# Layer 0 of a linear-attention block: tiles 6 and 7 are turned by VectorE and DMA instead of TensorE

## The chip, the core and the metric

The kernel runs on one core of one Trainium2 chip. The metric is the device time of one execution in microseconds (us). Before the change the median of three runs is 867.65 us (867.58 to 867.68). A core has five engines that run their own instruction streams in order and wait for each other by semaphores: TensorE (PE in the profile, its weight loads shown as PEld), VectorE (DVE), ScalarE (ACT), GpSimd (POOL) and SyncE (SP). In this kernel nearly every DMA is issued from SP's queue (SPq in the profile), in program order.

## What is computed

Two layers, each an attention block and an MLP block on x of 2048 rows by 448 columns:

```python
for layer in range(2):
    n = layernorm(x);  q, k, v = n @ wqkv          # 16 heads of 28
    pq, pk = phi(q), phi(k)                        # t + 1 if t > 0 else exp(t), + 1e-6
    x = x + (pq @ (pk.T @ v) / (pq @ sum(pk))) @ wo    # per head
    n = layernorm(x)
    x = x + gelu(n @ w1 + b1) @ w2 + b2
```

All inputs are float32. The kernel keeps that precision by splitting each operand into a high part (rounded to fp32r) and a low part (the rest), and sums three products: high by high, high by low, low by high.

## The kernel before, in words

The rows are cut into 16 tiles of 128 (t = 0 to 15) and 4 blocks of 4 tiles. A layer has a first phase, `phase1`, which goes over the tiles and gathers pk and G = n.T @ pk; a short transition; then the MLP, into which the second half of the attention is woven. The order of all instructions is written by hand: each engine and each queue executes its share in the order in which the Python code emits it. The change touches only phase 1 of layer 0.

For a tile t phase 1 needs these steps, each a token in the strings of `STEPS` and `STEP` and a function of the same meaning:

- `a` (`stage_a`, lines 206 to 216): statistics of the row norm on VectorE, then an inverse root on GpSimd (`brs`).
- `n` (`stage_n`, line 423): normalise on VectorE, in place. If t < TURNED[l], ScalarE also copies the last 64 columns twice into a tail (line 427), which the TensorE transposes read.
- The tile must be turned so that the 448 columns lie on partitions. There are two ways. For t < TURNED[l], `T` (`stage_b`, `transpose_x`, line 259) makes four TensorE transposes into a PSUM bank, and `X` (`split_x`, lines 271 and 272) splits it: ScalarE writes the high part XH, VectorE the low part XL. For t >= TURNED[l], `v` or `tu` (`stage_t`, `turn`, lines 298 and 299) turns squares of 32 by 32 on VectorE into a buffer `sq` that holds two tiles. After the odd tile of the pair, `store_sq` (line 304) writes the buffer to DRAM. The token `sp` (`spread`, line 310) reads it back with four DMAs that put each square in its place, and `X` (`split_t`, lines 316 and 317) splits from SBUF. The four reads wait for the store.
- `K` (`stage_k`, line 334): 11 matmuls XH, XL by wk into `psk`. `kp`, `kh`, `kl` (lines 350 to 353, 492, 501, 508): phi, its high and low part, and the running sum `za`.
- `s` (lines 458 to 460): high and low part of the normalised tile in its own layout, `xnh` and `xnl`.
- `G` (`stage_g`, line 563): 11 matmuls for the tile before.
- `Q` (`stage_q`, line 334): 11 matmuls by wq into `psq`, for t up to 8 in this phase. `qp` (`stage_qphi`, lines 350 to 353, 536): phi of it, one step later, and a store. The PSUM banks of `psq` and of the TensorE transposes are the same two (tag `h`).
- `ld`: loads of x for later tiles; `bg`: one or two pieces of the MLP weights are loaded by SP and split by ScalarE and GpSimd (lines 381 to 393).

In step t the token `K` works on tile t, `T` and `X` on tile t + 1, `G` on tile t - 1, `Q` on tile t, and `qp` on the tile whose `Q` ended the step before. The default order of a step is `qp K T X s a kp n kh kl tu G bg Q ld sp`. Below, K(12) stands for the token K of tile 12, and so on. Step 3 begins on TensorE at 27.14 us with K(3), step 4 at 34.33, step 5 at 41.42, step 6 at 48.49, step 7 at 55.54, step 8 at 62.16, step 9 at 68.76, step 10 at 73.16, step 11 at 77.57 and step 12 at 81.98.

Before the change tiles 8 to 15 of layer 0 are turned by VectorE: tiles 8 and 9 in step 4, tile 10 in step 5, and so on to tile 15 in step 10. The store of a pair follows its odd tile; the spreads are issued at the end of steps 4, 6, 8 and 10; the splits X(8) and X(9) stand in steps 7 and 8, X(10) and X(11) in steps 9 and 10, X(12) in step 11.

`k_at`, `q_at` and `g_at` say at which of the 11 places of a group the products with a low part stand.

Of the kernel before, what the change touches and what calls it, by code (L numbers as in the profile page):

```python
# [22 lines left out]
def linear_attn_mlp_kernel(  # L23
# [12 lines left out]
    pe, act, dve, pool, sp = nc.tensor, nc.scalar, nc.vector, nc.gpsimd, nc.sync  # L36
# [8 lines left out]
    G = 112  # L45
# [37 lines left out]
    def load_x(l, t):  # L83
        xt[l, t] = t448("H", 8, f"x{l}_{t}")
        sp.dma_start(xt[l, t], x_d[l][t * 128:(t + 1) * 128, :])
# [161 lines left out]
    def block(key):  # L247
        if key not in blocks:
            blocks[key] = Block(APART if key[0] == "a" else 0)
        return blocks[key]  # L250
# [3 lines left out]
    def transpose_x(xn, tail, key, j, tag="m"):  # L254

        block(key)
        tp = tps[key, j] = bank(tag, 4 if tag == "acc" else 2, "tp")
        for c in range(4):
            pe.transpose(tp[:, c * 128:(c + 1) * 128], xn[:, c * 128:(c + 1) * 128] if c < 3 else tail, ident)
# [8 lines left out]
    def split_x(key, j):  # L268
        tp = tps.pop((key, j))
        hi, lo = blocks[key].pieces(j)  # L270
        act.copy(hi, tp)
        dve.tensor_sub(lo, tp, f(hi))
# [20 lines left out]
    def turn(x, key, t):  # L293
        x = x[:, :D]
        if (key, t // 2) not in squares:
            squares[key, t // 2] = half("sq")
        sq = squares[key, t // 2].rearrange("p (m c u n) -> p c m u n", m=4, c=4, n=32)[:, :, :, t % 2]
        dve.transpose(sq[:, :3], x[:, :TL].rearrange("p (c m n) -> p c m n", c=3, n=32))
        dve.transpose(sq[:, 3].rearrange("p (u m) n -> p u m n", u=2),
                      x[:, TL:].rearrange("p (m n) -> p m n", n=32)[:, None].to_broadcast([128, 2, 2, 32]))  # L300
# [56 lines left out]
    def bg_pieces():  # L357
        n = 0
        both = []

        def stage():
            nonlocal n
            n += 1
            if n <= LATE:
                k = (n - 1) // 2
                if k % 2 == 0 or k > 5:
                    return t512("xn", 2, "stg")[:, :D]

                if n % 2:
                    both.append(half("stg"))  # L370
                return both[-1][:, n % 2 * 512:][:, :D]
            return t448(f"W{5 + n % 2}", 1, "stg")

        for fc in range(4):
            sl = slice(fc * D, (fc + 1) * D)
            for c in range(4):
                s = stage_piece(w1[:, sl], c, sp, stage())

                def go(c=c, s=s, sl=sl):
                    if c < 3:  # L380
                        act.copy(w1h[:, c, sl], s)
                        pool.tensor_tensor(w1l[:, c, sl], s, f(w1h[:, c, sl]), op=OP.subtract)
                    else:
                        act.copy(w1x[:, sl], s)
                        pool.tensor_tensor(w1x[64:128, sl], s[64:128], f(w1x[64:128, sl]), op=OP.subtract)
                yield go
        for i in range(NF):
            s = stage()
            sp.dma_start(s, w2[i * 128:(i + 1) * 128, :])

            def go(i=i, s=s):
                act.copy(w2h[:, i], s)
                pool.tensor_tensor(w2l[:, i], s, f(w2h[:, i]), op=OP.subtract)
            yield go

    bg = bg_pieces()
# [14 lines left out]
    sts = {}  # L411


    TURNED = (8, 0)
    tails = {}

    def stage_a(l, t):
# [2 lines left out]
    def stage_n(l, t):  # L420
# [3 lines left out]
        xns[l, t] = xs  # L424
        if t < TURNED[l]:
            d = tails[l, t] = b2b[:, t % 2 * 128:][:, :128]
            act.copy(d.rearrange("p (u n) -> p u n", u=2), xs[:, None, TL:].to_broadcast([128, 2, 64]))

    def stage_t(l, t):
        if t >= TURNED[l]:  # L430
            turn(xns[l, t], ("a", l, t // 4), t % 4)
            if t % 2:
                store_sq(("a", l, t // 4), t % 4 // 2)

    def stage_sp(l, t):
        if t >= TURNED[l]:
            block(("a", l, t // 4))
            spread(("a", l, t // 4), t % 4 // 2)

    def stage_b(l, t, tag="h"):  # L440
        if t < TURNED[l]:
            transpose_x(xns[l, t], tails.pop((l, t)), ("a", l, t // 4), t % 4, tag)
# [4 lines left out]
    def stage_x(l, t):  # L447
        key = ("a", l, t // 4)
        if t < TURNED[l]:
            split_x(key, t % 4)  # L450
# [13 lines left out]

    def k_at(l, t):
        if t < 9:
            return (3, 6, 9, 11) if t == 0 or l == 0 and 2 < t < 8 else (2, 5, 8, 11)
        return (2, 5, 8, 11) if t == 9 else (1, 4, 7, 10)

    def q_at(l, t):  # L470
        if t < 9:
            return (2, 5, 8, 11) if l == 0 and t < 7 else (2, 4, 7, 10) if t == 0 else (1, 4, 7, 10)
        return {11: (4, 7, 10, 11), 12: (5, 7, 9, 11),
                13: (5, 8, 10, 11), 15: (1, 5, 8, 11)}.get(t, (1, 4, 7, 10))

    def g_at(l, t):
        if t < 9:
            return (4, 7, 10) if l == 0 and 0 < t < 6 else (3, 6, 9)
        return (2, 5, 8) if t < NT - 1 else (2, 6, 9)

    def stage_k(l, t, cs=range(4)):
        ko[l, t] = proj("k", ("a", l, t // 4), t % 4, ko.get((l, t)), cs, k_at(l, t))
# [41 lines left out]
    def stage_q(l, t, cs=range(4), tag=None):  # L524
        if tag:
            qs_[l, t] = bank(tag, 4, "psq")[:, :D]
        qs_[l, t] = proj("q", ("a", l, t // 4), t % 4, qs_.get((l, t)), cs, q_at(l, t))
        if 3 in cs:
            qo.append((l, t, qs_.pop((l, t))))

    def stage_qphi(n=9):
        for _ in qo[:n]:
            l, t, o = qo.pop(0)

            e = phi(o, "eq", tag="e" if t < NT - 2 else "E")
            sp.dma_start(pq_d[l][t * 128:(t + 1) * 128, :], e)

    def fill_qphi():

        l, t, o = qo.pop(0)  # L540
        e = t512("e", 3, "eq")[:, :D]
        p = t512("E", 2, "ep")[:, :D]
        act.activation(e, o, AF.Relu, scale=-1.0)
        act.activation(p, o, AF.Relu)
        act.activation(e, e, AF.Exp, scale=-1.0)
        pool.tensor_tensor(e, p, e, op=OP.add)
        sp.dma_start(pq_d[l][t * 128:(t + 1) * 128, :], e)

    def stage_g(l, t, acc, mid=lambda: None):
        h, lo = split.pop((l, t))  # L550
        kh, kl = ks.pop((l, t))
        first, last = t == 0, t == NT - 1
        x = [h[:, c * 128:(c + 1) * 128] for c in range(3)] + [h[:, TL:]]
        his = [(c, x[c], k) for c in range(4) for k in (kh, kl)]
        if t == NT - 3:
            his = his[::2] + his[1::2]
        los = [(c, lo[:, c * 128:(c + 1) * 128], kh) for c in range(3)]
        made = merge(his, los, g_at(l, t))
        for i, (c, w, k) in enumerate(made):
            if i == 3:  # L560
                mid()
            others = [m[0] for m in made[:i]], [m[0] for m in made[i + 1:]]
            pe.matmul(acc[c], w, k, start=first and c not in others[0], stop=last and c not in others[1])  # L563
# [19 lines left out]
    STEP = "qp K T X s a kp n kh kl tu G bg Q ld sp"  # L583
    STEPS = {
# [9 lines left out]
    }  # L594
# [117 lines left out]
    def trans_gt(tr, acc):  # L712
        tr.gt = []
        for c in range(4):
            s = t512("A" if c < 2 else "B", 2, "gt")[:, :D]
            act.copy(s, acc[c])
            tr.gt.append(s)
# [52 lines left out]
    def load_pq(l, b, j):  # L770
        t = b * 4 + j
        pqt[l, t] = t448(f"W{j}", 1, f"pq{l}_{t}")
        sp.dma_start(pqt[l, t], pq_d[l][t * 128:(t + 1) * 128, :])
# [245 lines left out]
    for l in range(LAYERS):  # L1019
# [11 lines left out]
        def pre(j):  # L1031
# [6 lines left out]
            Q=lambda j: stage_q(l, fill.pop(0)), Qp=lambda j: fill_qphi(), Qv=lambda j: stage_qphi(j or 9),  # L1038
            Qa=lambda j: stage_q(l, fill.pop(0), tag="acc"), G=lambda j: stage_g(l, NT - 1, acc, lambda: trans_z(tr, zs[l])),
            ld=lambda j: (load_pq(l, 0, j), load_x(l, j)), gt=lambda j: trans_gt(tr, acc),  # L1040
# [14 lines left out]
        for b in range(NB):  # L1055
# [6 lines left out]
            for i in range(NF):  # L1062
# [12 lines left out]
                elif l + 1 < LAYERS:  # L1075
# [4 lines left out]
                    if i in (3, 4, 6, 7, 8):  # L1080
                        t = (3, 4, 6, 7, 8).index(i)
# [36 lines left out]
```

## Time and profile before

| | |
|---|---|
| median of three runs | 867.65 us |
| profiled execution | 867.87 us, of which the span is 866.1 us |
| TensorE matmul busy | 861.0 us, 99% of the span |
| VectorE, ScalarE, GpSimd busy | 494.3, 344.0, 216.5 us |
| granted TensorE clock | 1.00 |
| DMA | 94.76 MB, 109 GB/s mean |

The profile gives times from the start of the span; the 1.77 us between the span and the execution's own time lie around it. A row of the timeline has the start, the duration, the engine, the line of the kernel, the operation, output and input, how many instructions were merged into the row, and in brackets how long the engine had stood idle before it and who released it. Matmuls overlap, so that the pitch from one start to the next, and not the duration, is what one of them costs.

### The profile page before, as it was taken

Reading aid. Unit: us, or ns where it says so; the run is one execution under the profiler, and the core shown is the slowest. Engines: PE = TensorE matmul, PEld = TensorE weight load, DVE = VectorE, ACT = ScalarE, POOL = GpSimd, SP = SyncE. Lnnn points to the kernel's source line nnn. Section 1 sums busy time; section 2 is a strip of 40 time slices with the busy share of each in tenths; the row PEclk is TensorE's granted clock in tenths of the full one; section 3 lists DMA queues with packets and bytes.
Section 4 is the critical chain, followed back from the end, with each engine's and each line's share of the span. In section 5 each row is a group of like instructions: output and inputs, shape, how many; then the busy total and the mean of one; then the engine's idle time right before and its main releaser. Section 6 shows DMA issues by size and latency. Waiting matters only on the chain.

```text
span 866.1 us, 11660 instructions
## 1 busy us (share of the span) xinstructions
PE 861.0 (99%) x4181; PEld 771.3 (89%) x4181; DVE 494.3 (57%) x962; ACT 344.0 (40%) x604; POOL 216.5 (25%) x246
## 2 busy tenths in 40 slices
PE   9999999999999999999999999999999999999998
PEld 8999988888888888888899998988888888888887
DVE  7888596659456443226477876864674483533112
ACT  6776635334323322333356665432232233223231
POOL 5566522235013112012222343120220140140000
PEclk9999999999999999999999999999999999999999
DMA  5475636533313402051146443252332423111001
GB/s 160 139 235 177 192 89 215 184 105 116 134 60 107 156 0 98 1 181 49 49 141 194 164 129 107 100 189 81 113 109 92 135 71 116 50 49 43 0 1 43
DMA packets 63642, 94.76 MB, mean 109 GB/s; under 512 B 8928, under 2 KB 58720, under 8 KB 63584
## 3 DMA queue, kind: packets, MB, share of 16 engines
q1 hardware_dynamic: 63408, 93.87, 33.6%
q8 instruction: 33, 0.54, 0.2%
q14 instruction: 25, 0.20, 0.1%
q10 hardware_dynamic: 176, 0.14, 0.0%
HBM read 56.17 MB, written 34.60 MB: 105 GB/s over the span
## 4 chain that ended last, share of the span: by engine, by line
PE 98%; DMA 0%; DVE 0%; ACT 0%; POOL 0%; issue 0%; SPq 0%; DVEq 0%; ACTq 0%
PE hp L889 32%; PE y L919 10%; PE y L918 10%; PE y L920 10%; PE G L563 8%; PE psq L334 8%; PE psk L334 8%; PE op L827 2%; PE op L826 2%; PE op L828 2%; PE op L816 1%; PE op L815 1%; PE op L817 1%; PE kvp L724 1%; PE mp L734 1%; PE op L830 1%
## 5 line engine op out<-in xcount | busy, mean ns | idle before, releaser
L895 DVE TENSOR_TENSOR gl<-g,gh 128x512 fp32r<-128x512 f32 x112 | 83.2, 743 | 293.5 <-ACT gh L894 293.5
L891 ACT ACTIVATE g<-hp,b1s 128x512 f32<-128x512 f32 x112 | 77.2, 689 | 399.9 <-PE hp L889 395.4
L919 PE MATMUL y<-w2l,gh 128*128 128x448 f32 x447 | 163.6, 366 | 0.0
L918 PE MATMUL y<-w2h,gh 128*128 128x448 f32 x447 | 162.0, 362 | 0.0
L920 PE MATMUL y<-w2h,gl 128*128 128x448 f32 x447 | 160.1, 358 | 0.0
L889 PE MATMUL hp<-XH,w1l 128*128 128x512 f32 x336 | 130.7, 389 | 0.0
L889 PE MATMUL hp<-XH,w1h 128*128 128x512 f32 x336 | 130.7, 389 | 0.0
L889 PE MATMUL hp<-XL,w1h 128*128 128x512 f32 x336 | 130.1, 389 | 0.0
L216 POOL TENSOR_TENSOR brs<-bve,mhalf 128x1 f32<-128x1 f32 x64 | 39.5, 617 | 281.7 <-DVE bve L214 281.3
L918 PEld LDWEIGHTS y<-w2h,gh 128*128 128x128 f32 x447 | 83.7, 187 | 9.4
L919 PEld LDWEIGHTS y<-w2l,gh 128*128 128x128 f32 x447 | 83.9, 188 | 7.0
L920 PEld LDWEIGHTS y<-w2h,gl 128*128 128x128 f32 x447 | 84.0, 188 | 5.1 <-DVE gl L895 0.2
L889 PEld LDWEIGHTS hp<-XL,w1h 128*128 128x128 f32 x336 | 63.1, 188 | 13.1
L889 PEld LDWEIGHTS hp<-XH,w1h 128*128 128x128 f32 x336 | 63.0, 187 | 10.7
L889 PEld LDWEIGHTS hp<-XH,w1l 128*128 128x128 f32 x336 | 63.1, 188 | 9.9
L894 ACT CAST gh<-g 128x512 fp32r<-128x512 f32 x112 | 69.7, 623 | 3.6
L334 PE MATMUL psk<-wk,XH 128*128 128x448 f32 x210 | 61.8, 364 | 0.0
L334 PE MATMUL psq<-wq,XH 128*128 128x448 f32 x210 | 61.3, 366 | 0.0
L777 POOL TENSOR_TENSOR pz<-pq,zb 128x448 f32<-128x448 f32 x32 | 36.9, 1155 | 90.8 <-DVE dn L783 69.3
L459 POOL TENSOR_TENSOR xnl<-x,xnh 128x384 fp32r<-128x384 f32 x32 | 34.9, 1091 | 69.8 <-ACT xnh L458 56.4
L563 PE MATMUL G<-kh,xnh 128*128 128x448 f32 x128 | 46.8, 368 | 0.0
L563 PE MATMUL G<-kl,xnh 128*128 128x448 f32 x128 | 46.0, 365 | 0.0
(164 smaller groups left out, 1487.8 us busy)
## 6 DMA issues: line engine op xcount, KB each, us to landing
x<-in_A_x_dram SPq DMA_DIRECT2D x32, 224.0 KB, 3.5
pq_d<-eq SPq DMA_DIRECT2D x32, 224.0 KB, 2.7
pq<-pq_d SPq DMA_DIRECT2D x32, 224.0 KB, 3.2
sq_m<-sq SPq DMA_DIRECT2D x14, 512.0 KB, 2.7
sp<-sq_m SPq DMA_DIRECT2D x56, 128.0 KB, 2.8
x<-x_d SPq DMA_DIRECT2D x32, 224.0 KB, 3.3
sq_a<-sq SPq DMA_DIRECT2D x12, 512.0 KB, 2.9
sp<-sq_a SPq DMA_DIRECT2D x48, 128.0 KB, 2.8
```

The source lines that it names most:

```text
L216: pool.tensor_tensor(rs, ve, mhalf, op=OP.pow)
L334: pe.matmul(o, x, p, start=(i == 0), stop=(i == 10))
L459: pool.tensor_tensor(lo[:, :TL], xn[:, :TL], f(h[:, :TL]), op=OP.subtract)
L563: pe.matmul(acc[c], w, k, start=first and c not in others[0], stop=last and c not in others[1])
L777: pool.tensor_tensor(pz, pqt[l, b * 4 + j], tr.zb, op=OP.mult)
L889: pe.matmul(o, w, r, start=(k == 0), stop=(k == len(made) - 1))
L891: act.activation(g, hp, AF.Gelu_apprx_tanh, bias=b1s[:, i:i + 1])
L894: act.copy(gh, g)
L895: dve.tensor_sub(gl, g, f(gh))
L918: pe.matmul(acc[j], gh[:, s], w2h[:, i], start=first, stop=False)
L919: pe.matmul(acc[j], gh[:, s], w2l[:, i], start=False, stop=False)
L920: pe.matmul(acc[j], gl[:, s], w2h[:, i], start=False, stop=stop)
```

## The change

The limit from which on layer 0's tiles are turned by VectorE goes from 8 to 6. Tiles 6 and 7 lose their eight transposes on TensorE (in steps 5 and 6) and their tails. They are normalised in steps 2 and 3, turned at the end of VectorE's step 3, stored, and spread at the end of step 3. To make room, most later turns move: tile 9 from step 4 to 5, 10 from 5 to 6, 11 from 6 to 7, 12 from 7 to 8, 13 from 8 to 9, 14 from 9 to 10; the spreads of the pairs (8, 9), (10, 11) and (12, 13) move from the ends of steps 4, 6 and 8 to those of 5, 7 and 9. The splits X stay where they were. The places of the low products of a few tiles follow: of K for tiles 6 and 7, of Q for 5 and 6, of G for 4 and 5.

```diff
-    TURNED = (8, 0)
+    TURNED = (6, 0)
...
-            return (3, 6, 9, 11) if t == 0 or l == 0 and 2 < t < 8 else (2, 5, 8, 11)
+            return (3, 6, 9, 11) if t == 0 or l == 0 and 2 < t < 6 else (2, 5, 8, 11)
...
-            return (2, 5, 8, 11) if l == 0 and t < 7 else (2, 4, 7, 10) if t == 0 else (1, 4, 7, 10)
+            return (2, 5, 8, 11) if l == 0 and t < 5 else (2, 4, 7, 10) if t == 0 else (1, 4, 7, 10)
...
-            return (4, 7, 10) if l == 0 and 0 < t < 6 else (3, 6, 9)
+            return (4, 7, 10) if l == 0 and 0 < t < 4 else (3, 6, 9)
...
-        (0, 2): "K T X s a4 kp n4 a5 kh kl n5 a6 G bg Q ld",
-        (0, 3): "qp K T X s a7 kp kh n6 kl a8 G bg Q ld",
-        (0, 4): "qp K T X s a9 kp kh n7 n8 kl n9 v8 v9 G bg Q ld sp",
-        (0, 8): "qp K T X s a kp n kh kl tu a14 G bg Q ld sp",
-        (0, 9): "qp K T X s kp n14 kh kl v14 G bg",
-        (0, 10): "K T X s a15 kp n15 kh kl v15 G bg sp",
+        (0, 2): "K T X s a4 kp n4 a5 kh kl n5 a6 n6 G bg Q ld",
+        (0, 3): "qp K T X s a7 kp kh n7 kl v6 v7 G bg Q ld sp",
+        (0, 4): "qp K T X s a8 kp kh n8 a9 kl v8 G bg Q ld",
+        (0, 5): "qp K X s n9 a10 kp kh kl v9 n10 G bg Q ld sp",
+        (0, 6): "qp K X s a11 kp n11 kh kl v10 G bg Q ld sp",
+        (0, 7): "qp K X s a12 kp n12 kh kl v11 G bg Q ld sp",
+        (0, 8): "qp K X s a13 kp n13 kh kl v12 a14 G bg Q ld sp",
+        (0, 9): "qp K X s kp n14 kh kl v13 G bg sp",
+        (0, 10): "K X s a15 kp n15 kh kl v14 v15 G bg sp",
```

## The prediction

> **What bounds the kernel now.** I read the page's chain of work first, then the stretches of phase 1, then the timeline of each engine there.
>
> ```profile
> span 866.1 us, 11660 instructions
> ...
> PE 98%; DMA 0%; DVE 0%; ACT 0%; POOL 0%; issue 0%; SPq 0%; DVEq 0%; ACTq 0%
> ```
>
> The chain that ended last is TensorE for 98%: matmuls run back to back. What TensorE no longer executes is gained whole, and what makes it wait is lost whole, as long as nothing behind it has a wait to give back. The other engines count only where a tile reaches TensorE late. In phase 1 they are close to that; this is the stretch of step 11 (busy time of PE, PEld, DVE, ACT, POOL, then clock, DMA share, GB/s):
>
> ```profile
> 77.60:82.00 4.40, 4.40 (x24) 4.11 (x23) 4.18 (x10) 3.17 (x6) 2.04 (x3) 1.00 0.07 28
> ```
>
> TensorE needs all of the 4.40 us, VectorE 4.18 of them. A later turn therefore can't count on slack.
>
> **The change, part by part.**
>
> *Eight transposes go.* TensorE in step 5, and the same place in step 7, which has no transposes:
>
> ```profile
> 43.63 0.49 PE L259 MATMUL tp<-ident,x 128*128 128x128 f32 x3
> 43.96 0.27 PE L259 MATMUL tp<-ident,b2b 128*128 128x128 f32 x1
> 43.98 0.45 PE L563 MATMUL G<-kh,xnh 128*128 128x448 f32 x1
> 44.27 0.37 PE L563 MATMUL G<-kl,xnh 128*128 128x448 f32 x1
> ...
> 57.55 0.36 PE L334 MATMUL psk<-wk,XL 128*128 128x448 f32 x1
> 57.75 0.37 PE L563 MATMUL G<-kh,xnh 128*128 128x448 f32 x1
> ```
>
> From the first transpose to the second G matmul pass 0.64 us; a matmul without transposes ahead passes in 0.20. So a tile's transposes cost 0.44 us, and two tiles 0.88. That is the gain.
>
> *Tile 6 is normalised a step earlier (n6 at the end of step 2).* On VectorE it now stands ahead of phi of q of tile 2, which frees the PSUM bank that Q(3) writes. Rows of GpSimd, VectorE and TensorE in order of time, and two of step 4 for comparison:
>
> ```profile
> 30.49 0.55 POOL L216 TENSOR_TENSOR brs<-bve,mhalf 128x1 f32<-128x1 f32 x1 [1.93 <-DVE bve L214]
> 31.01 1.16 POOL L382 TENSOR_TENSOR w1l<-stg,w1h 128x448 fp32r<-128x448 f32 x1
> 31.30 0.62 DVE L353 SCALAR_TENSOR_TENSOR eq<-psq,eq 128x448 f32<-128x448 f32 x1 [0.95 <-ACT eq L351]
> 32.02 0.43 PE L334 MATMUL psq<-wq,XH 128*128 128x448 f32 x1
> ...
> 41.90 1.16 POOL L385 TENSOR_TENSOR w1x<-stg,w1x 64x448 fp32r<-64x448 f32 x1
> 42.38 0.93 DVE L423 TENSOR_SCALAR x<-x,bmv,brs 128x448 f32<-128x448 f32 x1
> ...
> L423 DVE TENSOR_SCALAR x<-x,bmv,brs x32: 504/512/1324, 5.4 to 498.6; 128x448 f32<-128x448 f32 x32
> ```
>
> Q(3) starts 0.10 us after phi ends at 31.92: no margin. n6 can't start before tile 6's root ends at 31.04. Alone it takes 0.51 us and phi starts at about 31.55, 0.25 late. But GpSimd's split of a weight starts at 31.01 and runs to 32.17, and the normalise of 42.38, which met such a split (41.90 to 43.06), took 0.93 us and ended 0.25 after it. By that n6 ends at 32.42 and phi is 1.1 us late. I take 1.0, since GpSimd's row starts first, and keep 0.25 as the other end. The Trainium skill (SBUF — State Buffer, Who interferes with whom) says that a VectorE operation using two ports and a GpSimd operation lock each other out, and that the one issued first holds the ports to its end. The row of 42.38 agrees; by this rule too the stall is the upper value, by a plain instruction count it would be the lower.
>
> *VectorE's step 3 gains two turns and loses a8.* Rows of VectorE at the end of step 3, and one turn of step 4:
>
> ```profile
> 35.77 0.62 DVE L206 BATCH_NORM_STATS2 bst<-x 128x6 f32<-128x448 f32 x1
> 36.42 0.18 DVE L212 BATCH_NORM_AGGREGATE bmv<-bst 128x2 f32<-128x6 f32 x1
> 36.64 0.15 DVE L214 TENSOR_SCALAR bve<-bmv 128x1 f32<-128x1 f32 x1
> ...
> 43.91 0.53 DVE L298 STREAM_TRANSPOSE sq<-x 128x384 f32<-128x384 f32 x1
> 44.37 0.27 DVE L299 STREAM_TRANSPOSE sq<-x 128x128 f32<-128x128 f32 x1
> ```
>
> The step's VectorE work ended at 36.79. Without a8 (35.77 to 36.79, 1.02 us), with two turns of 0.73 and the delay of n6 (0.25 to 1.1), tile 7's turn ends at 37.5 to 38.3.
>
> *The hand-over of a pair.* What follows a turn is one chain: store, wait for it, four reads, split on ScalarE, split on VectorE, first matmul. Before the change it is seen bare for the pair (14, 15), where ScalarE waited for the read. Rows of VectorE, SP's queue, ScalarE and TensorE:
>
> ```profile
> 75.25 0.27 DVE L299 STREAM_TRANSPOSE sq<-x 128x128 f32<-128x128 f32 x1
> 80.62 0.27 DVE L299 STREAM_TRANSPOSE sq<-x 128x128 f32<-128x128 f32 x1
> 80.91 0.32 SPq L304 DMA_DIRECT2D sq_a<-sq  x1
> 83.89 1.75 SPq L310 DMA_DIRECT2D sp<-sq_a  x4
> 88.17 0.62 ACT L316 CAST XH<-sp 128x512 fp32r<-128x512 f32 x1 [0.85 <-DMA sp<-sq_a]
> 88.83 0.69 DVE L317 TENSOR_TENSOR XL<-sp,XH 128x512 fp32r<-128x512 f32 x1 [0.76 <-ACT XH L316]
> ...
> 81.98 0.37 PE L334 MATMUL psk<-wk,XL 128*128 128x448 f32 x1
> ...
> DMA to landing us min/median/max: 2.5/2.9/3.7
> ```
>
> From the turn's end (80.89) to XH 7.28 us, from XH to the end of XL 1.35, and 0.1 to TensorE. The last row is of the four reads of all pairs, from issue to landing: a hand-over may be 0.3 shorter or 0.8 longer. The row of 81.98 is K(12), and it begins with the low part. Tile 13, the second of its pair, takes in step 9 the place that tile 14 had, whose turn ended at 75.52. Then XH(12) comes at 82.80 and K(12) can start at 84.25: 2.27 us after the time at which TensorE wants it. So even with everything else in time the change loses here more than it gained. The earlier pairs have room by the same count only if their own turns aren't late, which is the next step.
>
> *The chain from pair to pair.* ScalarE and VectorE work in order, so a late read of one pair holds back their step, and with it the turn that closes the next pair. Rows of ScalarE (the splits X(6), X(8), X(10)), VectorE (the ends of the turns of steps 5 and 7) and TensorE (K(8), K(10)):
>
> ```profile
> 44.27 0.59 ACT L271 CAST XH<-tp 128x512 fp32r<-128x512 f32 x1 [0.98 <-PE tp L259]
> 49.48 0.27 DVE L299 STREAM_TRANSPOSE sq<-x 128x128 f32<-128x128 f32 x1
> 57.07 0.61 ACT L316 CAST XH<-sp 128x512 fp32r<-128x512 f32 x1
> 62.43 0.27 DVE L299 STREAM_TRANSPOSE sq<-x 128x128 f32<-128x128 f32 x1
> 70.08 0.61 ACT L316 CAST XH<-sp 128x512 fp32r<-128x512 f32 x1
> ...
> 62.16 0.37 PE L334 MATMUL psk<-wk,XH 128*128 128x448 f32 x1
> ...
> 73.16 0.36 PE L334 MATMUL psk<-wk,XL 128*128 128x448 f32 x1
> ```
>
> I go along it with the 7.28 of a hand-over. Tile 7's turn ends at 37.5 to 38.3, so XH(6) starts at 44.8 to 45.6 (before: 44.27). From there to the end of the step's turn passed 5.48 us; n9, now ahead of it, adds 0.5 to 0.9: tile 9's turn ends at 50.8 to 52.0, XH(8) starts at 58.1 to 59.3 (before: 57.07), in time for K(8). From XH(8) to the end of the step's turn passed 5.63: tile 11's turn ends at 63.7 to 64.9, XH(10) starts at 71.0 to 72.2 (before: 70.08); K(10) at 73.16 is met just about. From XH(10) to the turn's end at 75.52 passed 5.44: tile 13's turn ends at 76.4 to 77.6, XH(12) at 83.7 to 84.9, K(12) at 85.2 to 86.4. Steps with Q last long enough on TensorE for the chain to keep up; steps 9 and 10 have no Q (4.40 us each) and do not. The 0.88 of gain and the stall at Q(3) don't enter by themselves: K(12) starts when its tile comes. TensorE is then 3.2 to 4.4 us later than before. I take 3.5, near the lower end, as VectorE's waits in step 3 and after can swallow some tenths.
>
> *The rest, costed at nothing.* The pair (14, 15) is stored some 0.7 us later, but K(14) moves by more. SP issues the store and four reads of tiles 6 and 7 ahead of two weight pieces, the load of x of tile 10 and the store of phi: the weight splits of step 4 come some 1 to 2 us later on ScalarE, behind them phi of q of tile 4, which VectorE takes up only at about 44.5; if that cover fails, Q(5) is late by what is left, and that again is swallowed at K(12). The turns use two more of the five shared buffers, each of which its last reader has left by then. The two missing tails lighten ScalarE. The changed places of low products alter no matmul's 0.20 us.
>
> **The rivals.**
>
> *The lateness isn't handed on.* If the pairs up to (10, 11) arrive so early that they hold nobody back, only the bare hand-over of (12, 13) is left: 2.27 late, less 0.88, plus 0.25 to 1.1 at Q(3) ahead of it: 869.3 to 870.2. For it: K(8) has room. Against: XH(8) and XH(10) come after the times of before by my count, by 1.0 to 2.1 us.
>
> *Not slower: K(12) finds its tile.* This is one mechanism: the hand-over of (12, 13) takes at most 5.0 us in place of 7.28, or tile 13 is turned before 73.3. Then the gain stands against Q(3) alone: -0.88 + 0.25 to 1.1, 867.0 to 867.9. For it: the stretch around it moves few bytes (28 GB/s in the row above). Against: the wait for the store alone is 2.98 us by the rows, and a read never landed in under 2.5. Between this and the rival above lie 867.9 to 869.3.
>
> *More than that: the gap slows what follows.* If TensorE, after standing still at K(12), ran at half pace for as long as one step (4.40 us), that would add up to 4.40: 873 to 875.5. Against: the granted clock is 1.00 in every stretch of phase 1 that I read. The Trainium skill (TensorE: Matmul & The Clock Gate, What's actually happening) halves the clock after an idle window of about 3.4 us; my gap is shorter, and by that page such a window would cost some 1.7 us. The same place is reached if the split XL(10), XL(11) or XL(12) meets GpSimd more often.
>
> **How the numbers follow.** The profiled execution took 867.87 us, 1.77 more than its span, and lies 0.22 above the median. 866.1 + 3.5 + 1.77 is 871.4 for it; against the median of 867.65 the prediction is 871.1. A change of 0.2% is 1.74 us, about what a measurement of this kernel can tell from no change; so slower begins at 869.4. Chances: the chain 0.62 (870.2 to 872.9: 3.2 to 4.4 late, some tenths of shorter or longer reads on each side), lateness not handed on 0.14, between that and no wait 0.08, no wait at K(12) 0.07, more than that 0.09. Slower: 0.62 + 0.13 + 0.09 = 0.84; same: 0.14; faster: 0.02, since the whole gain of 0.88 is half of what would count. The likeliest case alone spans 870.2 to 872.9; the range of 868.8 to 873.0 leaves out the gain and most of the last rival, some 0.17.
>
> **What the profile afterwards would show.** TensorE waits at K(12) for XL, itself behind ScalarE's wait for `sp<-sq_a` of 1 us and more, and a gap of 2 to 3 us there; a smaller one at Q(3), with a normalise of about 1.3 us ahead of it; ScalarE waiting for the read at X(6), X(8) and X(10) too; no transposes of tiles 6 and 7. MLP and layer 1 as long as before. The prediction is wrong if ScalarE finds the reads of (8, 9) and (10, 11) landed, or if the hand-over of (12, 13) is far from 7.28 us.

## The result and the profile after

The changed kernel takes 875.28 us (median of 4 runs, 875.07 to 876.11) against 867.64 us beside it: a ratio of 1.0091 [1.0078, 1.0104], so 7.6 us slower. The direction was as forecast; the size is twice the forecast 3.5, and the time lies outside the range. The profiled execution took 875.14 us with a span of 873.4; before, the span was 866.1.

First the page's chain of work and the three waits that matter in phase 1 (waiting engine, tile and line, who released it, then total us, times, longest):

```profile
PE 90%; DMA 3%; DVE 3%; POOL 1%; issue 1%; SPq 1%; ACT 1%; DVEq 0%; POOLq 0%; ACTq 0%
...
PE psk L334 <- DVE XL L317: 3.6, 1, 3.6
PE psq L334 <- DVE eq L353: 0.8, 1, 0.8
ACT XH L316 <- DMA sp<-sq_a: 8.6, 4, 2.9
```

TensorE's share of the chain fell from 98% to 90%. The rest now runs through DMA, VectorE, SP's queue and ScalarE: the way of a tile from its turn to its split. ScalarE waits for the reads four times. TensorE waits once for 3.6 us, and that isn't at K(12). Its timeline:

```profile
32.85 0.47 PE L334 MATMUL psq<-wq,XH 128*128 128x448 f32 x1 [0.81 <-DVE eq L353]
...
51.57 0.47 PE L563 MATMUL G<-kl,xnh 128*128 128x448 f32 x1 [0.17 <-DVE kl L501]
...
77.44 0.74 PE L334 MATMUL psk<-wk,XL 128*128 128x448 f32 x1 [3.59 <-DVE XL L317]
84.62 0.36 PE L334 MATMUL psk<-wk,XL 128*128 128x448 f32 x1
89.03 0.47 PE L334 MATMUL psk<-wk,XL 128*128 128x448 f32 x1
```

These are Q(3), G of step 6, and K(10), K(11) and K(12). K(10) comes 4.28 us later than before (73.16) and K(12) 7.05 later (81.98). Between K(10) and K(11) lie 7.18 us instead of 4.41, without a wait. The table by stretches says why (busy time of PE, PEld, DVE, ACT, POOL, then clock, DMA share, GB/s):

```profile
73.20:77.60 4.40, 0.81 (x5) 0.42 (x3) 3.35 (x6) 2.11 (x4) 2.37 (x3) 0.86 0.63 208
77.60:82.00 4.40, 4.40 (x12) 3.97 (x13) 4.27 (x8) 2.12 (x5) 3.92 (x5) 0.50 0.16 67
82.00:86.40 4.40, 4.40 (x20) 4.03 (x20) 3.64 (x10) 2.17 (x4) 1.71 (x2) 0.87 0.71 213
```

After the stand the granted clock is 0.50 for a whole stretch, and TensorE does 12 matmuls in the time for 20 and more. From TensorE's side the 7.05 us add up as follows. Up to K(9) it is 0.52 late (69.28 instead of 68.76): the stall at Q(3) and short stands at G, less what was gained. From K(9) to K(10) it loses 3.76, from K(10) to K(11) 2.77. From K(11) to K(12) it loses nothing (4.41 both times).

The same instant can be reached from the tile's side. These are the ends of the pairs' turns on VectorE, and then ScalarE's splits X(6), X(8), X(10) and X(12):

```profile
37.79 0.27 DVE L299 STREAM_TRANSPOSE sq<-x 128x128 f32<-128x128 f32 x1
52.45 0.27 DVE L299 STREAM_TRANSPOSE sq<-x 128x128 f32<-128x128 f32 x1
65.84 0.27 DVE L299 STREAM_TRANSPOSE sq<-x 128x128 f32<-128x128 f32 x1
80.19 0.27 DVE L299 STREAM_TRANSPOSE sq<-x 128x128 f32<-128x128 f32 x1
```

```profile
46.23 0.62 ACT L316 CAST XH<-sp 128x512 fp32r<-128x512 f32 x1 [1.89 <-DMA sp<-sq_a]
60.74 0.62 ACT L316 CAST XH<-sp 128x512 fp32r<-128x512 f32 x1 [1.15 <-DMA sp<-sq_a]
75.11 0.62 ACT L316 CAST XH<-sp 128x512 fp32r<-128x512 f32 x1 [2.86 <-DMA sp<-sq_a]
87.63 0.62 ACT L316 CAST XH<-sp 128x512 fp32r<-128x512 f32 x1 [2.73 <-DMA sp<-sq_a]
```

The hand-overs from a turn's end to XH are 8.17, 8.02, 9.00 and 7.17 us. From XH to the next turn's end pass 6.49, 5.37 and 5.35, and from XH(12) to K(12) 1.40. Tile 12 is ready just as TensorE, slowed, arrives. So there are two explanations of the same 89.03: the chain of tiles, or a stand followed by half pace. One of them must be idle, and the experiments decide which.

Outside phase 1 nothing changed: the first matmul of the MLP starts at 143.44 instead of 136.27, 7.17 later, and from there to the end of the span pass 730.0 us after and 729.8 before. So nearly all of the 7.3 us between the two spans is the lateness of K(12).

### The profile page after: what moved, and what is told of

Its sections match the earlier page's. It is cut to its first block, busy times and chain, and to the rows that moved or that the text cites. A ratio compares the mean times of both kernels' runs of the same rounds, so it can differ in the third digit from the quotient of the medians.

```text
span 873.4 us, 11661 instructions
## 1 busy us (share of the span) xinstructions
PE 863.0 (99%) x4173; PEld 771.9 (88%) x4173; DVE 497.9 (57%) x966; ACT 343.7 (39%) x602; POOL 216.8 (25%) x246
## 4 chain that ended last, share of the span: by engine, by line
PE 90%; DMA 3%; DVE 3%; POOL 1%; issue 1%; SPq 1%; ACT 1%; DVEq 0%; POOLq 0%; ACTq 0%
PE hp L892 32%; PE y L922 10%; PE y L921 10%; PE y L923 10%; PE G L563 6%; PE psq L334 6%; PE psk L334 6%; PE op L830 2%; PE op L829 2%; PE op L831 2%; DMA sp<-sq_a 1%; DMA sq_a<-sq 1%; PE op L819 1%; PE op L818 1%; PE op L820 1%
## 5 line engine op out<-in xcount | busy, mean ns | idle before, releaser
L317 DVE TENSOR_TENSOR XL<-sp,XH 128x512 fp32r<-128x512 f32 x54 | 46.4, 868 | 5.9 <-ACT XH L316 5.9
L334 PE MATMUL psk<-wk,XL 128*128 128x448 f32 x120 | 44.2, 369 | 3.6 <-DVE XL L317 3.6
```

Of the source, the lines that this page charges most:

```text
L317: eng.tensor_tensor(lo.rearrange("p (c i n) -> p c i n", c=4, n=32), x, f(h), op=OP.subtract)
L334: pe.matmul(o, x, p, start=(i == 0), stop=(i == 10))
```

## The experiments

All short diffs are against the changed kernel unless another is named. Ratios are against the kernel before, run on the same chip.

**1. Fill the gap at K(10).** Idle matmuls keep TensorE busy while it waits, in the bank that K(10) overwrites.

```diff
+        if (l, t) == (0, 10):
+            ko[l, t] = bank("m", 2, "psk")[:, :D]
+            for i in range(16):
+                pe.matmul(ko[l, t][:, :128], ident, ident, start=True, stop=True)
```

> The changed kernel with 16 idle matmuls (identity by identity, 128x128 float32) on TensorE ahead of K(10), in the bank that K(10) overwrites; they fill the 3.59 us for which it stood still. Theory 'clock': the gap itself stays (K(10) starts at about 77.4 us as before), but the granted clock stays at 1.00, the matmuls from 77.4 to 83.2 us go at their 0.20 us pitch and not 0.37, and the time falls by 2.5 to 3 us, to 872.3 to 872.8, with a new wait at K(12), whose tile comes at about 88.3, taking some of it back (K(12) is then wanted at about 86): 873.5 to 875 at the least favourable. Rival 'the gap is all': the slow stretch is something that follows the late tile (late operands, bank conflicts), the pitch stays at 0.37 and the time at 875.3.

Measured: 875.74 us (875.61 to 875.87), ratio 1.0088 [1.0068, 1.0108]. TensorE's row of K(12), and the stretch that had run at half pace:

```profile
89.02 0.44 PE L334 MATMUL psk<-wk,XL 128*128 128x448 f32 x1 [2.18 <-DVE XL L317]
```

```profile
77.60:82.00 4.40, 4.40 (x24) 4.07 (x24) 4.17 (x8) 3.20 (x6) 3.77 (x5) 1.00 0.18 74
```

The clock stays at 1.00 and the pace is full, yet K(12) starts at 89.02, as it did at 89.03: what was saved is waited for. The time, expected at 875 at most with the full pace, doesn't fall. The low clock behind K(10) had no price. The chain of tiles sets K(12).

**2. Shorten the hand-over in SP's queue.** The weight pieces and the load of x are issued ahead of the store, not between it and its reads.

```diff
-        (0, 3): "qp K T X s a7 kp kh n7 kl v6 v7 G bg Q ld sp",
+        (0, 3): "qp K T X s a7 kp kh n7 bg ld kl v6 v7 G Q sp",
-        (0, 5): "qp K X s n9 a10 kp kh kl v9 n10 G bg Q ld sp",
+        (0, 5): "qp K X s n9 a10 kp kh bg ld kl v9 n10 G Q sp",
-        (0, 7): "qp K X s a12 kp n12 kh kl v11 G bg Q ld sp",
+        (0, 7): "qp K X s a12 kp n12 kh bg ld kl v11 G Q sp",
-        (0, 9): "qp K X s kp n14 kh kl v13 G bg sp",
+        (0, 9): "qp K X s kp n14 kh bg kl v13 G sp",
```

> The change with SP's loads of weight pieces and of x in steps 3, 5, 7 and 9 issued ahead of the store of the pair, not between the store and its reads; nothing else moves. Theory 'the loads lengthen the hand-over': turn end to XH falls from 8.2, 8.0 and 9.0 us for the pairs (6,7), (8,9) and (10,11) to 7.0 to 7.5; XH(10) starts at 71 to 72.5 in place of 75.1, K(10) waits under 1 us, and K(12) then waits 2.5 to 3.5, as had been predicted: 870.5 to 872.5, or about 874 if that second gap lowers the clock. Rival 'the hand-over is as long as it is whatever stands in the queue': 8 to 9 us remain, 874.5 to 876.

Measured: 873.86 us (873.35 to 874.37), 1.0067 [1.0046, 1.0087]. First SP's queue and the summary of the reads of pair (10, 11) in the changed kernel, then the reads of pair (6, 7) here, then X(6), X(8), X(10), X(12) here:

```profile
66.14 0.33 SPq L304 DMA_DIRECT2D sq_a<-sq  x1
66.53 0.48 SPq L103 DMA_DIRECT2D stg<-in_B_w_dram  x1
67.07 0.65 SPq L104 DMA_DIRECT2D stg<-in_B_w_dram  x1
67.81 0.53 SPq L101 DMA_DIRECT2D stg<-in_B_w_dram  x1
68.44 0.38 SPq L85 DMA_DIRECT2D x<-in_A_x_dram  x1
69.13 2.53 SPq L310 DMA_DIRECT2D sp<-sq_a  x4
...
DMA to landing us min/median/max: 3.8/4.7/5.0
```

```profile
DMA to landing us min/median/max: 2.6/2.8/2.9
```

```profile
44.85 0.62 ACT L316 CAST XH<-sp 128x512 fp32r<-128x512 f32 x1 [1.38 <-DMA sp<-sq_a]
58.22 0.62 ACT L316 CAST XH<-sp 128x512 fp32r<-128x512 f32 x1
71.72 0.62 ACT L316 CAST XH<-sp 128x512 fp32r<-128x512 f32 x1 [1.83 <-DMA sp<-sq_a]
85.25 0.62 ACT L316 CAST XH<-sp 128x512 fp32r<-128x512 f32 x1 [4.23 <-DMA sp<-sq_a]
```

In the changed kernel four loads stand between a store and its reads, and the reads land in 3.8, 3.7 and 4.7 us (medians of the first three pairs). With one load between, as for (12, 13), or none, as for (6, 7) here, it is 2.8. What the reads meet is seen in the 2 us from the first read on (columns as above, so the DMA share is the last but one). These are the reads of (6, 7) and (12, 13) in the changed kernel, and then those of (6, 7) here:

```profile
41.00:43.00 2.00, 2.00 (x11) 1.88 (x11) 1.93 (x6) 1.23 (x3) 0.40 (x1) 1.00 0.96 280
83.40:85.40 2.00, 2.00 (x11) 1.85 (x10) 1.71 (x4) 1.09 (x2) 0.43 (x1) 1.00 0.45 136
40.60:42.60 2.00, 2.00 (x12) 1.87 (x11) 1.73 (x6) 1.83 (x4) 0.37 (x2) 1.00 0.35 104
```

Behind four loads the DMA engines are busy for 0.96, 0.96 and 0.91 of the time in which the reads begin (first three pairs of the changed kernel); here, with none between, it is 0.33 to 0.38 for all four pairs. The hand-over of (6, 7) is 6.88 (turn end 37.97, XH 44.85) and that of (8, 9) at most 6.88, as XH(8) waits for no read. The third is 7.96: its reads still took 4.0, though nothing stands between and the DMA share at their start is as low (0.37). Loads follow right behind its reads, but behind those of the first two pairs too, so the cause is open. The last is 8.19: a weight load was issued at 76.92, just ahead of its store, and from that store to its first read pass 3.66 us (77.34 to 81.00), where the other three have 2.6. K(10) is now in time at 73.12, and K(12) starts at 86.65 after 3.28 us of waiting, 2.38 earlier than in the changed kernel. The time falls by only 1.4. In this stretch of its profile (columns as above) the clock is low behind K(12), where no later wait absorbs it; from K(12) to G pass 3.22 us (86.65 to 89.87) and from there to K(13) 2.91 (to 92.78), instead of some 2.2 each, so that about 1.7 of the 2.38 are lost again:

```profile
88.00:91.00 3.00, 3.00 (x10) 2.65 (x9) 2.20 (x3) 2.56 (x6) 2.95 (x4) 0.50 0.46 129
```

**3. The statistics of tile 14 a step later.** Ahead of X(10) VectorE runs the norm statistics of tile 14 (`a14`). Does that hold back the tile?

```diff
-        (0, 8): "qp K X s a13 kp n13 kh kl v12 a14 G bg Q ld sp",
-        (0, 9): "qp K X s kp n14 kh kl v13 G bg sp",
+        (0, 8): "qp K X s a13 kp n13 kh kl v12 G bg Q ld sp",
+        (0, 9): "qp K X s a14 kp n14 kh kl v13 G bg sp",
```

> The changed kernel with the norm statistics of tile 14, for whose x VectorE stood still for 2.34 us ahead of X(10), moved from step 8 to step 9, behind X(10). Theory 'XL(10) waits for its read': XH(10) still starts at about 75 us, VectorE now waits for ScalarE there, K(10) is reached at 76.4 to 77.4 and the time stays within 874.5 to 876. Rival 'the late load of x is what held K(10)': K(10) at about 75 or earlier, and the time 2 us lower.

Measured: 876.0 us (875.4 to 876.6), 1.0095 [1.0077, 1.0113]. K(10) and K(12):

```profile
76.49 0.47 PE L334 MATMUL psk<-wk,XL 128*128 128x448 f32 x1 [1.89 <-DVE XL L317]
...
88.99 0.74 PE L334 MATMUL psk<-wk,XL 128*128 128x448 f32 x1 [2.26 <-DVE XL L317]
```

K(10) comes 0.95 earlier, since VectorE's part of the split (XL(10)) took 0.69 instead of 1.62 us, and K(12) doesn't move. That extra at XL(10) is not what delays K(12).

**4. Tile 6 normalised in step 3, behind phi of q.** This takes the stall at Q(3) away.

```diff
-        (0, 2): "K T X s a4 kp n4 a5 kh kl n5 a6 n6 G bg Q ld",
-        (0, 3): "qp K T X s a7 kp kh n7 kl v6 v7 G bg Q ld sp",
+        (0, 2): "K T X s a4 kp n4 a5 kh kl n5 a6 G bg Q ld",
+        (0, 3): "qp K T X s a7 kp kh n6 n7 kl v6 v7 G bg Q ld sp",
```

> The changed kernel with the normalising of tile 6 back in step 3, behind phi of q of tile 2 and of k of tile 3. The wait of 0.81 us at Q(3) goes. Theory 'K(12) starts when its tile comes': the time falls only by what the chain of turns starts earlier, 0 to 0.5 us (874.8 to 875.6). Rival 'each wait of TensorE adds up by itself': 0.8 us lower, 874.3 to 874.6, with K(12) 0.8 us earlier.

Measured: 876.03 us (875.46 to 876.61), 1.0095 [1.0077, 1.0114]. Q(3) starts at 31.82 without a wait, and still:

```profile
88.92 0.47 PE L334 MATMUL psk<-wk,XL 128*128 128x448 f32 x1 [1.87 <-DVE XL L317]
```

The 0.81 us at Q(3) were real and worth nothing, but it isn't K(12) that takes them back. K(6) starts at 47.74 instead of 48.83, and the gain ends in that step. Tile 7's turn ends at 37.02, 1.04 earlier than in the changed kernel, and X(6) starts no earlier:

```profile
46.23 0.62 ACT L316 CAST XH<-sp 128x512 fp32r<-128x512 f32 x1 [2.23 <-DMA sp<-sq_a]
```

The hand-over of (6, 7) took 9.21 instead of 8.17 with the same four loads; why is open. TensorE then stands 0.80 at G of step 6, and K(7) is at 55.88, where the changed kernel has it at 55.87. In both kernels, this and the one before, TensorE now stands right ahead of K(12) and the clock is 0.50 from 90 to 92 us, which fits their being slightly slower than the changed kernel and not faster.

**5. The moved turns without tiles 6 and 7, first form.** The limit goes back to 8 with the new places of the turns and of `n6` and `n7`.

```diff
-    TURNED = (6, 0)
+    TURNED = (8, 0)
-        (0, 3): "qp K T X s a7 kp kh n7 kl v6 v7 G bg Q ld sp",
+        (0, 3): "qp K T X s a7 kp kh n7 kl v6 v7 G bg Q ld",
```

> The other half of the change alone: tiles 6 and 7 by TensorE as before the change, and the turns of tiles 9 to 14 a step later as in the change. Theory 'the moved turns cost it': tile 13's turn in step 9 comes at 75.5 us or later and its hand-over takes 7.3 to 9.0 us, so K(12) waits at least 2.3 us, and K(10) up to 1.5 more: 870.5 to 873; above 874 only if TensorE stands still for over 3 us at one place and its clock falls. Rival 'turning tiles 6 and 7 at all': below 868.5, with the loss only where both come together.

Measured: 879.33 us (878.41 to 880.25), 1.013 [1.0109, 1.015]. This doesn't do one part alone. Tiles 6 and 7 have tails again, now written so early that they take the buffers of the tails of tiles 4 and 5 before these are transposed, which changes values, and the transposes of tile 4 wait 2.19 us for a tail. It tells nothing on the dispute.

**6. The moved turns alone.** Against the kernel before:

```diff
-        (0, 4): "qp K T X s a9 kp kh n7 n8 kl n9 v8 v9 G bg Q ld sp",
-        (0, 8): "qp K T X s a kp n kh kl tu a14 G bg Q ld sp",
-        (0, 9): "qp K T X s kp n14 kh kl v14 G bg",
-        (0, 10): "K T X s a15 kp n15 kh kl v15 G bg sp",
+        (0, 4): "qp K T X s a9 kp kh n7 n8 kl n9 v8 G bg Q ld",
+        (0, 5): "qp K T X s a10 kp n10 kh kl v9 G bg Q ld sp",
+        (0, 6): "qp K T X s a11 kp n11 kh kl v10 G bg Q ld sp",
+        (0, 7): "qp K T X s a12 kp n12 kh kl v11 G bg Q ld sp",
+        (0, 8): "qp K T X s a13 kp n13 kh kl v12 a14 G bg Q ld sp",
+        (0, 9): "qp K T X s kp n14 kh kl v13 G bg sp",
+        (0, 10): "K T X s a15 kp n15 kh kl v14 v15 G bg sp",
```

> The kernel before, tiles 6 and 7 turned by TensorE and normalised where they were, with only the later turns and spreads moved a step later as in the change (tile 9 in step 5, 10 in 6, up to 14 with 15 in step 10; spreads in steps 5, 7, 9, 10). Theory 'the moved turns start a chain, each link a hand-over of 8.0 and 9.0 us for the pairs (8,9) and (10,11) and 7.2 for (12,13), as the changed kernel showed': tile 9's turn ends at about 49.8, XH(8) 57.8, XH(10) 72.2, XH(12) 84.7, K(12) at about 86.1 in place of 81.98: 871 to 872.5 (some 1.5 more if the clock falls in that gap). With 7.28 us a link only the last one is late: K(12) at 84.3, 869.5 to 870.3. Rival 'it takes the turning of tiles 6 and 7': below 868.5.

Measured: 873.76 us (873.29 to 874.23), 1.0069 [1.0051, 1.0088]. TensorE around K(12), and the clock there by stretches:

```profile
86.01 0.74 PE L334 MATMUL psk<-wk,XL 128*128 128x448 f32 x1 [2.53 <-DVE XL L317]
...
89.63 0.37 PE L563 MATMUL G<-kh,xnh 128*128 128x448 f32 x1
```

```profile
84.00:85.00 1.00, 0.00 (x0) 0.00 (x0) 0.00 (x0) 0.39 (x1) 0.00 (x0) 1.00 0.98 401
85.00:86.00 1.00, 0.00 (x0) 0.00 (x0) 0.69 (x1) 0.97 (x3) 0.00 (x0) 0.72 0.99 288
87.00:88.00 1.00, 1.00 (x4) 0.91 (x3) 0.35 (x1) 1.00 (x3) 1.00 (x2) 0.50 0.58 161
89.00:90.00 1.00, 1.00 (x6) 0.92 (x6) 0.85 (x1) 0.23 (x2) 1.00 (x2) 1.00 0.35 93
```

Without a single tile more turned by VectorE, about four fifths of the loss are there (873.76 against 867.73 beside it, 6.0 of 7.6 us). Part of that is the clock, which cost the changed kernel nothing: K(12) is at 86.01, 4.03 late (of 7.05), and then its 11 matmuls take 3.62 us in place of some 2.2, because the clock falls in the gap. The hand-overs are 8.19, 8.81 and 7.45 (ends of turns 49.46, 63.01, 77.16). Tiles 6 and 7 put one more link ahead of the same chain, and K(12) goes from 86.01 to 89.03.

**7. Fill the gap at K(12) of that kernel.** Twelve idle matmuls ahead of K(12), against the kernel of experiment 6:

```diff
+        if (l, t) == (0, 12):
+            ko[l, t] = bank("m", 2, "psk")[:, :D]
+            for i in range(12):
+                pe.matmul(ko[l, t][:, :128], ident, ident, start=True, stop=True)
```

> The kernel before with only the turns moved a step later, and 12 idle matmuls (identity by identity, 128x128 float32) ahead of K(12), in the bank that K(12) overwrites; they fill the 2.53 us gap after which the clock was 0.50 for some 3.5 us. K(12) starts at about 86.0 as without them. Theory 'the low clock has a price where nothing waits behind it': K(12) takes 2.2 us and not 3.6, and the time falls by 1.3 to 1.5, to about 872 (without them 873.3 and 874.2). Rival 'as at K(10), what follows takes it back': no change.

Measured: 872.8 us (871.91 to 873.69), 1.0057 [1.0039, 1.0074]; about 872 was expected. The intervals of the two kernels overlap, so one profile of each has to decide. The stretch that had run at half pace:

```profile
86.00:87.00 1.00, 1.00 (x7) 0.92 (x6) 0.60 (x1) 0.76 (x2) 0.53 (x1) 1.00 0.09 9
```

G behind K(12) starts at 87.98 instead of 89.63, 1.65 earlier, of which 0.35 is K(12) itself (85.66 instead of 86.01); the span is 870.2 instead of 871.5. By these two profiles the low clock costs about 1.3 us where no later wait absorbs it, and nothing where one does (experiment 1).

**8. The later turns back in their old places, tiles 6 and 7 still turned.**

```diff
-        (0, 6): "qp K X s a11 kp n11 kh kl v10 G bg Q ld sp",
-        (0, 7): "qp K X s a12 kp n12 kh kl v11 G bg Q ld sp",
-        (0, 8): "qp K X s a13 kp n13 kh kl v12 a14 G bg Q ld sp",
-        (0, 9): "qp K X s kp n14 kh kl v13 G bg sp",
-        (0, 10): "K X s a15 kp n15 kh kl v14 v15 G bg sp",
+        (0, 6): "qp K X s a11 kp n11 kh kl v10 v11 G bg Q ld sp",
+        (0, 7): "qp K X s a12 kp n12 kh kl v12 G bg Q ld",
+        (0, 8): "qp K X s a13 kp n13 kh kl v13 a14 G bg Q ld sp",
+        (0, 9): "qp K X s kp n14 kh kl v14 G bg",
+        (0, 10): "K X s a15 kp n15 kh kl v15 G bg sp",
```

> Tiles 6 and 7 turned as in the change, but from step 6 on the turns and spreads are back at their old places: tiles 10 and 11 both turned in step 6, 12 in 7, 13 in 8, 14 in 9, 15 in 10, spreads at the ends of steps 6, 8 and 10. Theory 'the turns that come a step later cost the time': no wait at K(10) and K(12), no low clock; left are the gain of 0.88 and the waits of 0.81 at Q(3) and 0.17 at G(5): 867.6 to 868.3. Rival 'turning tiles 6 and 7 at all costs the time' (their store and reads delay the pairs behind): XH(10) still waits for its read and the time stays above 870.

Measured: 870.17 us (869.1 to 870.56, 10 runs), 1.0024 [1.0014, 1.0033]. Five of the 7.6 us are gone and K(12) starts at 84.09 instead of 89.03, without a wait, which is the main point. The expected 867.6 to 868.3 didn't come: 0.82 us stay at Q(3), and K(10) waits for XL(10):

```profile
72.93 0.63 DVE L206 BATCH_NORM_STATS2 bst<-x 128x6 f32<-128x448 f32 x1 [1.10 <-DMA x<-in_A_x_dram]
75.14 0.48 PE L334 MATMUL psk<-wk,XL 128*128 128x448 f32 x1 [1.10 <-DVE XL L317]
```

The read isn't late: XH(10) starts at 72.10 without a wait. VectorE, which has the statistics of tile 14 ahead of XL(10), stands 1.10 us for x of tile 14 and begins XL(10) only at 74.41. K(10) is 1.98 later than before the change and K(12) 2.11.

**9. Everything in time.** The old places, tile 6 normalised behind phi of q, and the loads ahead of the store.

```diff
+        (0, 2): "K T X s a4 kp n4 a5 kh kl n5 a6 G bg Q ld",
+        (0, 3): "qp K T X s a7 kp kh n6 n7 bg ld kl v6 v7 G Q sp",
...
+        (0, 5): "qp K X s a10 kp kh n9 bg ld kl v9 n10 G Q sp",
+        (0, 6): "qp K X s a11 kp n11 kh bg ld kl v10 v11 G Q sp",
+        (0, 7): "qp K X s a12 kp n12 kh bg ld kl v12 G Q",
+        (0, 8): "qp K X s a13 kp n13 kh bg ld kl v13 a14 G Q sp",
+        (0, 9): "qp K X s kp n14 kh kl v14 G bg",
+        (0, 10): "K X s a15 kp n15 kh kl v15 G bg sp",
```

> Tiles 6 and 7 turned by VectorE as in the change, but so that each pair is in time: n6 back behind phi of q of tile 2 (in step 3), n9 behind phi of k, tiles 10 and 11 both turned in step 6 and from there on all turns and spreads at their old places, and SP's loads in steps 3, 5, 6, 7 and 8 issued ahead of the stores. Theory 'the saved transposes are worth 0.88 us once nothing waits': no wait of TensorE at Q(3), G, K(10) and K(12), 866.6 to 867.4 against 867.7 to 867.9 of the kernel before, so 0.4 to 1.0 faster. Rival 'VectorE has no room for two more turns at any place': a wait at some G or K of 0.5 us and more, 868 to 870.

Measured: 868.14 us (866.67 to 869.14, 11 runs), 0.9999 [0.999, 1.0008]: no difference, where 0.4 to 1.0 faster was expected. TensorE needs 13.22 us from K(5) to K(7) instead of 14.12, so the 0.90 us of the eight transposes are there, and it reaches K(9) at 67.64, 1.1 us before the old 68.76 (0.15 of it because K(3) starts earlier). Then it waits 0.91 us at K(10). VectorE shows for what:

```profile
70.89 0.63 DVE L206 BATCH_NORM_STATS2 bst<-x 128x6 f32<-128x448 f32 x1 [2.86 <-DMA x<-in_A_x_dram]
```

VectorE stands 2.86 us for x of tile 14, with XL(10) behind it in its order. K(10) starts at 73.11, as in the kernel before (73.16). SP's queue shows that the loads ahead of the store have a price too: from the store to the first read pass 4.11 us for (10, 11) and 5.75 for (12, 13), where the changed kernel has 2.9 to 3.0.

**10 and 11. Two ways around that wait**, both against the kernel of experiment 9. In the first `a14` stands in step 9 behind X(10), and in step 7 the loads of x come ahead of the weights. In the second x of tile 14 is loaded a step earlier.

```diff
-        (0, 7): "qp K X s a12 kp n12 kh bg ld kl v12 G Q",
-        (0, 8): "qp K X s a13 kp n13 kh bg ld kl v13 a14 G Q sp",
-        (0, 9): "qp K X s kp n14 kh kl v14 G bg",
+        (0, 7): "qp K X s a12 kp n12 kh ld bg kl v12 G Q",
+        (0, 8): "qp K X s a13 kp n13 kh bg ld kl v13 G Q sp",
+        (0, 9): "qp K X s a14 kp n14 kh kl v14 G bg",
```

> The version in which every pair is in time, with the one wait that was left in it mended: the norm statistics of tile 14 stand in step 9 behind X(10), so that VectorE no longer stands for x of tile 14 ahead of XL(10), and SP loads x of tile 14 ahead of the weight pieces of step 7. Theory 'the saved transposes are worth 0.88 us, plus what the waits at Q and G of before cost, once nothing waits': TensorE reaches K(10) 1.0 us earlier than in the kernel before and waits nowhere in phase 1, 866.5 to 867.0, that is 0.8 to 1.2 faster. Rival 'the same wait moves on' (x of tile 14 holds the norm, and with it K(11), K(12) or a G): the gain is under 0.4.

```diff
-                    load_to(l, NORM[l][t + 2][-1])
+                    load_to(l, NORM[l][t + 2][-1] + (l == 0 and t == 6))
```

> The version in which the pairs are in time, with the norm statistics of tile 14 in step 8 as there, but x of tile 14 loaded together with that of tile 13 in step 6, ahead of the store of the pair (10,11), so that VectorE does not stand for it ahead of XL(10). Theory 'the transposes saved are gained where nothing waits': TensorE reaches K(10) and K(13) some 1.0 us earlier than in the kernel before, counted from K(3): 866.6 to 867.3, 0.5 to 1.1 faster. Rival 'VectorE, GpSimd and the reads have no room for it and a wait of some tenths turns up at K(11), K(12) or G wherever one is mended': 867.4 to 868.6.

Measured: 868.64 us (867.99 to 871.4, 12 runs), 1.0014 [1.0005, 1.0022], and 869.48 us (869.14 to 871.16, 11 runs), 1.002 [1.0011, 1.0029]. In the first K(10) starts at 72.54 without a wait, but K(11) waits 0.47 for its split, XL(11), and K(12) is at 82.60, not earlier than before the change (81.98). In the second it is ScalarE's turn to stand:

```profile
69.97 0.57 ACT L384 CAST w1x<-stg 128x448 fp32r<-128x448 f32 x1 [3.92 <-DMA stg<-in_B_w_dram]
```

K(10) waits 0.86 and K(11) 0.47. In both cases the wait moved on to another load or tile, as the rivals had it; the second time is above even its rival's 868.6. No version tried was measurably faster than the kernel before.

## Why the prediction was right in kind and wrong in size

**The mechanism held.** K(12) starts when its tile comes, and stalls and gains of TensorE ahead of it don't enter: removing 0.95 us of lateness at K(10) (experiment 3) or the low clock (1) left K(12) at 88.99 and 89.02. The stall at Q(3) didn't enter either (4), though its removal was taken back in step 6 already. Moving the turns back (8) brought K(12) from 89.03 to 84.09 and took most of the loss away. The rival of the bare hand-over (869.3 to 870.2) is out: lateness is handed on, as the waits before X(6), X(8) and X(10) show. So is the rival "K(12) finds its tile": it needed a hand-over of (12, 13) of at most 5.0 us, and that took 7.17.

**The step that failed is the hand-over of 7.28 us**, "the hand-over of a pair", used four times. It was taken from the pair (14, 15), which had two loads between store and reads. The first three pairs have four. They measured 8.17, 8.02, 9.00 and 7.17, so the chain got 0.89 + 0.74 + 1.72 - 0.11 = 3.24 us longer than four times 7.28. K(12) had been forecast for 85.2 to 86.4, 85.8 in the middle; with 3.24 more it is 89.04, and it came at 89.03. That this fits to 0.01 is partly luck, since the other pieces missed by up to 0.3 and cancel. The 3.5 that the forecast took lies another 0.3 below that middle. The waits for the store were unchanged (2.99, 2.93, 2.99 and 2.89 from store to first read); nearly all of the excess lies behind the first read (5.15, 5.06, 5.98 and 4.25 us from there to XH, against 4.28 for the pair it was taken from). That the loads between are what lengthened it is shown for the first two pairs (experiment 2) and open for the third. The margin of 0.8 for longer reads was put on one hand-over and not on each of four, and a row of the trace before would have warned: there the reads of (10, 11), with three loads between, took 3.5/3.6/3.7 and those of (8, 9), also with three, 2.8/3.2/3.3, against 2.6/2.8/2.9 for (14, 15). The forecast's sign of being wrong, a hand-over of (12, 13) far from 7.28, looked at the one link of the four that held. Given the longer hand-overs, the forecast pieces between them held: 6.49 (forecast 5.98 to 6.41), 5.37 (5.63) and 5.35 (5.44), and 1.40 (1.45) at the end.

**"K(10) at 73.16 is met just about" failed with it.** XH(10) came at 75.11 instead of 71.0 to 72.2, and XL(10) behind it took 1.62 us beside a GpSimd split. K(10) waited 3.59. So the long gap of TensorE, forecast for K(12), stood at K(10), and at K(12) there was none.

**The gap and the clock.** The rival "the gap slows what follows" named the right time (873 to 875.5) and the right sign (clock 0.50), but not the cause of the time here: without the low clock the changed kernel takes 875.74. Its price, put at up to 4.40 us, was 2.77 of TensorE's time behind K(10), all absorbed at K(12), and about 1.3 in experiment 7, where it counts. In the kernel of experiment 2 it counts as well. By the rule quoted of the Trainium skill (TensorE: Matmul & The Clock Gate, What's actually happening), an idle window of about 3.4 us throttles the clock. The measurement differs: in the stand of 3.59, which began at 73.85, the clock was 0.83 from 76.0 to 76.5 and 0.50 behind that, so it fell after some 2.5 us, and stands of 1.87 to 2.53 lowered it too (experiments 3, 4 and 6).

**What came as forecast.** Q(3) waited 0.81 (0.25 to 1.1, taken 1.0), behind a normalise of tile 6 that took 1.34 us beside GpSimd (forecast about 1.3). The eight transposes are worth 0.90 us (0.88), shown in experiment 9. In the changed kernel itself only about half shows (K(5) to K(7) 13.66 instead of 14.12): in step 6 TensorE stands for the low part of phi of k, the row at 51.57. MLP and layer 1 are as long as before.

## What to carry to other kernels

Price a hand-over through DRAM from a row whose queue holds the same between store and reads, and carry its margin once for each link: in a chain of hand-overs the errors add. Ask of each store and read what the DMA engines still have to move when it is issued: loads between store and reads lengthened the reads here (the hand-over of (6, 7) took 8.17 to 9.21 us in the runs with four of them and 6.88 to 7.57 in those with none), and loads issued shortly ahead of a store delayed the store (3.66 to 5.75 us to its first read, instead of 2.6 to 3.0). Time gained on the engine that bounds the kernel shows only if the next thing it waits for comes earlier too; here 0.90 us were gained and given back at K(10) and K(11), where the loads in SP's order and the orders of VectorE and ScalarE set the tile.

## What the runs showed of the hardware

- The granted clock can fall in short stands of TensorE. In phase 1 it fell around stands of 1.87 and 2.38 (experiment 4), 2.19 and 2.46 (5), 2.26 (3), 2.53 (6), 3.28 (2) and 3.59 us (the changed kernel), and not around 0.91 (9), 1.10 (8), 1.74 (5, at K(10)), 1.89 (3, at K(10)) and 2.18 (1). Since 1.87 is on one side and 2.18 on the other, the length alone doesn't decide.
- The times of these changes lie on a grid. They can be worked out from the mean clock of stretches of half a us; these are the two falls of experiment 4 (clock in the third column from the end):

```profile
76.00:76.50 0.50, 0.00 (x0) 0.00 (x0) 0.50 (x1) 0.50 (x2) 0.29 (x1) 0.62 0.99 376
89.50:90.00 0.50, 0.50 (x4) 0.44 (x3) 0.37 (x1) 0.26 (x2) 0.27 (x1) 0.77 0.00 0
```

  A mean of 0.62 between 1.00 and 0.50 puts the first fall at 76.12, and 0.77 the second at 89.77: 13.65 us apart, which is four times 3.41. Each stretch at the low clock lasts 3.41 to 3.42 us, in the changed kernel 6.83 (76.33 to 83.16), and the two falls of experiment 5 lie 58.03 apart, 17 times 3.41. In the 3.41 us that end at a fall TensorE stood for 1.87 to 2.48 us, at all eight falls. The stand of 1.89 is cut by a point of its run's grid (75.17, counted back from the fall at 88.82) into 0.57 and 1.32, that of 1.74 into 0.22 and 1.52. So a fall goes with how much of one such window TensorE stands, with the limit somewhere between 1.52 and 1.87 us. This is read out of these traces and not tested, and the run with 2.18 has no fall to place its grid by.
- Four reads of 128 KB landed in 2.7 to 3.2 us (median of the four, all runs, phase 1 of layer 0 up to 92 us) with one or two loads between store and reads, in 3.2 to 3.6 with three, and in 3.5 to 4.7 with four. With none they took 2.7 to 3.4 and once 4.0 (experiment 2), so it is not the count of loads alone.
- XL, a VectorE operation with two operands in SBUF, took 0.69 us alone and 1.62 beside a GpSimd split; the normalise took 0.51 and 1.34. That agrees with the Trainium skill (SBUF — State Buffer, Who interferes with whom), by which a VectorE operation with two inputs in SBUF contends with a GpSimd operation that reads SBUF, and one in a mode that uses two ports with any. That the normalise is in such a mode no run shows.
